# Attention with a top-32 mask and a feed-forward block: heads turned a unit sooner, lasting halves, a plain second block

## The chip, the cores and the metric

The kernel runs on one core of one Trainium2 chip. The metric is the device time of one launch, in microseconds (us); the value given for a kernel is the median of several runs. A core has five engines that each take their instructions in order: TensorE (PE in the profile, with its weight loads as PEld), VectorE (DVE), ScalarE (ACT), GpSimd (POOL) and SyncE (SP), which here issues nearly all DMAs. Waits between engines are semaphores that a framework places from what each instruction reads and writes. The program order is the one in which the Python code calls the instructions: the kernel asks for a manual schedule.

## What is computed

Everything is 32-bit floating point. The shapes are B = 8 batches, H = 8 heads, S = 576 rows, D = 64 columns a head, 512 model columns, 2048 hidden columns; the two weight matrices arrive in 64-bit floating point.

```python
scores = scale * np.matmul(q, k.transpose(0, 1, 3, 2))
kth = np.partition(scores, -top_k, axis=-1)[..., -top_k:-top_k + 1]   # top_k = 32
scores = np.where(scores >= kth, scores, -1000000000.0)
scores = scores - np.max(scores, axis=-1, keepdims=True)
attn = np.exp(scores)
attn = attn / (np.sum(attn, axis=-1, keepdims=True) + 1e-09)
x = np.matmul(attn, v)                 # then (B, H, S, D) -> (B, S, H*D)
mu, var = mean and variance of x over its last axis
xn = (x - mu) / np.sqrt(var + 1e-06) * g_ln
out = x + np.maximum(xn @ w_ch1, 0.0) @ w_ch2
```

## The kernel before

**Units and steps.** A *job* is one pair of heads of one batch with one group of query rows; a *unit* is 128 query rows of a job for both heads (two tiles of 128 x 576 scores), or the last 64 rows of both heads in one tile (a *rest* unit). There are 160 units. The main loop has one *step* for each unit and some more behind them. In step n VectorE works on unit n; the scores of unit n + 2 are made on TensorE and copied to `sc` by ScalarE; unit n - 1 is masked (`prepare`, `mask`) and exponentiated (`weigh`); unit n - 2 is turned (`turn` on TensorE, or `move` by VectorE and two DMAs); and two to four steps after a group's last unit its value product follows (`values`, `take_values`, `place`).

**Selection.** `halve` (L413 on) writes the elementwise maximum of the two halves of a score row to `hi` (L425) and the minimum to `lo` (L426). `select(u, 0..3)` takes 8 maxima at a time from `hi` (L447) and strikes them out (L433); `select(u, 1)` first puts the 8 maxima of `lo` into columns 288 to 295 of `hi` (L439). `watch` (L466, GpSimd) compares column 295 of `hi` with the threshold, so that a second pass can be run if 8 were too few. `mask` is a Relu on ScalarE (L496) and a subtraction on GpSimd (L499) for each tile; `weigh` is the exponential (L507). `hi` comes from a pool of two buffers: `halve` of unit n takes the buffer of unit n - 2 and waits until that one is given back.

**Moved units.** `move` transposes 32 x 32 squares of the exponentials on VectorE into the unit's own `sc` buffer (L538) and sends it to DRAM (`turned`, L553) some fills later (`SEND_AGE`); three steps after the unit's own, `bring` fetches it in four DMAs to `pt` (L548), which the value product reads.

**Heads.** `load` brings q and k rows in 32-column pieces; `turn_heads` transposes them on VectorE (L331) to `kT`, `qT` and `late_qT`, two buffers each; `turns` says in which step. Jobs that come back to the same heads later (`twin`) fetch them from DRAM.

**Weights.** The 64-bit weights are rebuilt in 32 pieces in steps 0 to 20: `split` (ScalarE and GpSimd, L163 to L170), `shift` (VectorE, L176), `join` (two GpSimd operations, L182 and L184). Four pieces come ahead of step 0, then one a step, later two. A join of a step's pieces stands behind the mask in GpSimd's order, and the watch stands behind the join.

**The feed-forward blocks.** Rows of x become 18 *blocks* of 256 rows, given to a list `todo` (`give`) as their attention is finished. A block has rows to turn, 64 hidden matmuls of 256 columns (L779), and a projection. `plain` projects with 32 matmuls of 512 columns (L818). `seven` does it with seven products instead of eight (56 matmuls of 256 columns, L936), with sums of the hidden rows on GpSimd (L866 to L868, L872) and four combined weight quarters: two stay in `wt`, two (*forms*) are kept in DRAM and fetched into the right half of `w2` in turn (`fetch_form`). The combined quarters are made by `form_pair` (four GpSimd subtractions of 128 x 512, L990 to L993), four times, once block 0 is through; from then on `w2` no longer holds the plain weights. Block 0 is plain, the other 17 are seven.

**The planner.** A `fill` (eight of them a step) takes matmuls from the head of `todo` as long as the head may run and the share of the step isn't used up. Up to step 21 the share is what VectorE's modelled step exceeds TensorE's by. Later `slot` spreads the listed work evenly to every later `give`:

```python
for m in sorted(gives):
    if m > n:
        even = min(even, (left - RESERVE) / (m - n))
        left += sum(b.cost() for b in gives[m])
```

Gives come in steps 9, 20, 28, 36, 43, ... 136, 148, 149, 156, 163.

Of the kernel before, what the change touches and what calls it, by code (L numbers as in the profile page):

```python
# [10 lines left out]
ALU = mybir.AluOpType  # L11
# [18 lines left out]
def compute(  # L30
# [26 lines left out]
    def pool(name, bufs, **kw):  # L57
        return ctx.enter_context(tc.tile_pool(name=name, bufs=bufs, **kw))
# [7 lines left out]
    kqpool = pool("kq", 2)  # L66
    vpool = pool("v", NV)
    scpool = pool("sc", 5)
    hipool = pool("hi", 2)
    lopool = pool("lo", 1)  # L70
    epool = pool("e", 2)
    ptpool = pool("pt", 1)
# [18 lines left out]
    def const(shape, name):  # L91
        return consts.tile(shape, FP32, tag=name, name=name)
# [14 lines left out]
    if doubt is not None:  # L107
        watched = const([P, 2, 34], "watched")
        nc.gpsimd.memset(watched[:], -1.0)
    ident = const([P, P], "ident")  # L110
    make_identity(nc, ident[:])
    half = const([P, J], "half")
# [113 lines left out]
    def join_weights(n):  # L226
        for x in batches.get(n - 1, []):
            x.join()
# [184 lines left out]
    def halve(u):  # L413

        nt = len(u.tiles)  # L420
        u.lo = lopool.tile([P, 2, HALF], FP32, tag="lo", name="lo")
        u.hi = hipool.tile([P, 2, HALF + 8 * low_rounds], FP32, tag="hi", name="hi")
        a, b = u.sc[:, 0:nt, 0:HALF], u.sc[:, 0:nt, HALF:S]
        lo, hi = u.lo[:, 0:nt], u.hi[:, 0:nt, 0:HALF]
        nc.vector.tensor_tensor(hi, a, b, ALU.max)  # L425
        nc.vector.tensor_tensor(lo, a, b, ALU.min)  # L426
# [66 lines left out]
    def mask(u, t):  # L493
        if u.e is None:
            u.e = epool.tile([P, 2, S], FP32, tag="e", name="e")
        nc.scalar.activation(  # L496
            u.e[:, t], u.sc[:, t], AF.Relu, bias=u.edge[:, t : t + 1], scale=-STEEP
        )
        nc.gpsimd.tensor_tensor(u.e[:, t], u.e[:, t], u.sc[:, t], ALU.subtract)  # L499
# [186 lines left out]
    class Block:  # L686
# [41 lines left out]
            return sum(t[1] for part in self.items() for t in part)  # L728

        def items(self):  # L730
            return self.plain() if self is blocks[0] else self.seven()

        def turn_x(self, i):
            if i == 0:
# [70 lines left out]
        def plain(self):  # L805

            hs = {}
            ps = {}
            self.o = {}

            def run(h, bank):
                hs[h] = self.relu(bank)

            def project(i, f):
                if f == 0:
                    ps[i] = product("ops")
                at = f % 2 * 2 * P + i * P
                nc.tensor.matmul(  # L818
                    ps[i][:],
                    hs[f // 2][:, at : at + P],  # L820
                    w2[:, f, :],
                    start=(f == 0),
                    stop=(f == NF - 1),
                )
                if f == NF - 1:
                    o = self.o[i] = opool.tile([P, DM], FP32, tag="o", name="o")
                    nc.scalar.copy(o[:], ps[i][:])
                    self.finish(i)
                    if i == self.n - 1:
                        plain_done[0] = now[0]  # L830

            return (
                self.rows(),
                self.hidden_items(range(NF), lambda f: (f // 2, f % 2), run),
                [
                    (
                        "project",
                        PER_ROW * DM,
                        lambda i=i, f=f: project(i, f),
                        lambda f=f: done(ready[NF + f]) and (f < NF - 1 or self.ready),  # L840
                    )
                    for f in range(NF)
                    for i in range(self.n)
                ],
            )
# [115 lines left out]
                ],  # L961
            )

    PER_ROW = 1.71e-3
    SUM_AGE, END_AGE, FETCH_AGE, STORE_AGE, LOAD_AGE = 7, 6, 10, 8, 3
    SEND_AGE, CENTRE_AGE = 2, 6
    blocks = []
    plain_done, formed, used, fetched = [None], [None], [], [0]

    def close(blk):  # L970
        while blk.ends:
            blk.ends.pop(0)()
# [3 lines left out]
    def slot_of(i):  # L976
        return w2[:, 2 * i : 2 * i + 2, 2 * P : DM]

    def form_pair(i):

        lo, hi = slice(2 * i, 2 * i + 2), slice(NF // 2 + 2 * i, NF // 2 + 2 * i + 2)
        b11, b12 = w2[:, lo, 0 : 2 * P], w2[:, lo, 2 * P : DM]
        b21, b22 = w2[:, hi, 0 : 2 * P], w2[:, hi, 2 * P : DM]
        tt = nc.gpsimd.tensor_tensor
        x = xpool.tile([P, 2, DM], FP32, tag="x", name="form")
        t1, t2 = wt[:, 0, lo], wt[:, 1, lo]
        t4, t3 = (x[:, s].rearrange("p (f n) -> p f n", f=2) for s in range(2))
        tt(t1, b12, b11, ALU.subtract)  # L990
        tt(t2, b22, t1, ALU.subtract)
        tt(t3, t2, b11, ALU.subtract)
        tt(t4, b21, t2, ALU.subtract)  # L993
        return i, x

    def keep_pair(made):
        i, x = made
        for s in range(2):
            nc.sync.dma_start(scratch[:, s, i], x[:, s])
        if i == 3:  # L1000
            formed[0] = now[0]

    def fetch_form():
        m = fetched[0]
# [6 lines left out]
    def fetch_forms(age):  # L1011
        if done(formed[0]):
            free = 4 + sum(tick[0] - x >= age for x in used)
            while fetched[0] < min(free, 8 * (len(blocks) - 1)):
                fetch_form()

    def forms(blk, k, j):
        m = 8 * (blocks.index(blk) - 1) + 4 * k + j // 2
        while fetched[0] <= m:
            fetch_form()  # L1020
        return w2[:, j, 2 * P : DM]
# [110 lines left out]
    for j in jobs[1:]:  # L1132
        before = jobs[jobs.index(j) - 1]
        made = next(n for n in range(N) if units[j.first] in due(n))
        step = max(min(before.first, made - 1), 0)
        if j.twin:
            fetches.setdefault(max(step - 1, 0), []).append(j)
        else:
            turns[step] = j
            keeps[step + 1] = j  # L1140
# [47 lines left out]
        return u.i + u.group.lag + 1 if u and u.rest and u.job.b % 2 else None  # L1188

    recips, rows_of, ends_due = {}, {}, {}  # L1190
    pairs_left, made_pair = list(range(4)), []

    def arrived(n, key, x):
        blk, i = block_of[key]
# [20 lines left out]
    for n in range(END):  # L1215
# [31 lines left out]
        if mk:  # L1247
            prepare(mk)
            for t in range(len(mk.tiles)):
                mask(mk, t)  # L1250
        if n:
            join_weights(n)
        if mk and doubt is not None:
            watch(mk)
        if plain_done[0] is not None and plain_done[0] < n - 1:
            if made_pair:
                keep_pair(made_pair.pop())
            if pairs_left:
                made_pair.append(form_pair(pairs_left.pop(0)))
        for x in ahead:  # L1260
            take_scores(x)
        if g and not quick:
# [33 lines left out]
            keep_den(ex)  # L1296
        if u:
            select(u, 1)
        if n == gives_first:
            for blk, i in rows_of.pop(n):  # L1300
                blk.stats(i)
# [126 lines left out]
```

## Time and profile before

| | us |
|---|---|
| median of 3 runs | 1618.3 (1617.16 to 1620.39) |
| the profiled execution | 1617.0 |
| its span, first to last instruction | 1615.1 |
| busy: TensorE / VectorE / ScalarE / GpSimd | 1487.4 / 1371.2 / 1057.7 / 1033.9 |

The profile is of one execution. Its page gives each engine's busy time and a row of 40 equal slices (a digit is the busy share in tenths); the waits say which instruction stood idle and what ended that; the chain of waits is followed back from the last instruction. A line such as L425 is line 425 of the kernel before. A TensorE that is shown busy can still have small stalls, since the ends of matmuls are modelled.

### The profile page before, as it was taken

The page shows a single profiled execution, that of the slowest core. Times are in us where ns is not written, and L with a number is a line of the kernel's source. Part 1 is how long each engine was busy: PE and PEld are TensorE (multiplying, and loading weights), DVE is VectorE, ACT ScalarE, POOL GpSimd, SP SyncE. Part 2 cuts the span into 40 slices and gives each one's busy share as a digit, 9 for nine tenths or more (in the row PEclk, how much of TensorE's full clock was granted, in tenths as well). Part 3 has the DMA queues.
Part 4 walks back from the last instruction along what each step waited for, and adds up shares of the span by engine and source line. Part 5 has one row for each costly group of instructions (what it writes and reads, how often), then busy time and mean ns, then how long its engine had stood idle before and what let it go on. Part 6 is the DMA issues. An engine that isn't in the chain of part 4 may idle for free.

```text
span 1615.1 us, 27577 instructions
## 1 busy us (share of the span) xinstructions
PE 1487.4 (92%) x7954; PEld 1131.2 (70%) x7954; DVE 1371.2 (85%) x3979; ACT 1057.7 (65%) x2988; POOL 1033.9 (64%) x1513
## 2 busy tenths in 40 slices
PE   3578769799999999999999999999999999999997
PEld 2346436477777677777777777777777777778886
DVE  5997998899989997999978999999999999666100
ACT  5878866667677767776767576767676676454421
POOL 6968886957566565847565756484757475647614
PEclk9879879799999999999999999999999999999999
DMA  8424763556635675565753476546666554342411
GB/s 212 115 70 138 214 154 101 159 137 189 215 103 159 181 210 153 151 185 135 204 151 112 141 200 187 157 131 178 167 176 183 170 167 142 104 120 90 138 34 48
DMA packets 387561, 241.56 MB, mean 150 GB/s; under 512 B 263492, under 2 KB 355656, under 8 KB 387400
## 3 DMA queue, kind: packets, MB, share of 16 engines
q1 hardware_dynamic: 382664, 239.11, 52.0%
q8 instruction: 66, 1.08, 0.3%
q10 hardware_dynamic: 4736, 0.59, 0.2%
q14 instruction: 95, 0.78, 0.2%
HBM read 165.15 MB, written 74.45 MB: 148 GB/s over the span
## 4 chain that ended last, share of the span: by engine, by line
PE 51%; DVE 25%; POOL 10%; DMA 5%; ACT 5%; issue 2%; SPq 1%; ACTq 0%; DVEq 0%; POOLq 0%
PE hps L779 20%; PE ops L936 15%; DVE m L447 7%; DVE hi L433 6%; PE scps L404 6%; PE av L632 5%; POOL e L499 4%; DVE sc L538 3%; DVE lo L426 2%; DVE hi L425 2%; DVE hi L439 2%; DMA pt<-turned 2%; DMA turned<-sc 2%; PE av L639 2%; PE tp L565 2%
## 5 line engine op out<-in xcount | busy, mean ns | idle before, releaser
L499 POOL TENSOR_TENSOR e<-e,sc 128x576 f32<-128x576 f32 x288 | 408.1, 1435 | 444.6 <-ACT e L496 338.9
L779 PE MATMUL hps<-xT,w 128*128 128x256 f32 x2304 | 539.0, 384 | 5.2 <-ACT xT L741 3.1
L779 PEld LDWEIGHTS hps<-xT,w 128*128 128x128 f32 x2304 | 429.9, 192 | 70.0 <-issue 7.7
L447 DVE MAX8 m<-hi 128x8 f32<-128x296 f32 (+1 forms) x1152 | 470.1, 443 | 0.5
L433 DVE MATCH_REPLACE8 hi<-m,hi 128x288 f32<-128x288 f32 (+1 forms) x864 | 377.7, 442 | 0.0
L936 PE MATMUL ops<-w,h 128*128 128x256 f32 x1360 | 321.4, 382 | 2.8 <-POOL h L872 1.4
L936 PEld LDWEIGHTS ops<-w,h 128*128 128x128 f32 x1360 | 250.8, 191 | 40.5 <-issue 3.5
L496 ACT ACTIVATE e<-sc,m 128x576 f32<-128x576 f32 x288 | 209.3, 769 | 70.4 <-PE scps L599 69.6
L507 ACT ACTIVATE e<-e,m 128x576 f32<-128x576 f32 x288 | 226.8, 790 | 43.0 <-POOL e L499 41.8
L385 ACT COPY sc<-scps 128x288 f32<-128x288 f32 x576 | 187.9, 402 | 68.6 <-POOL e L499 50.6
L425 DVE TENSOR_TENSOR hi<-sc 128x576 f32<-128x576 f32 (+1 forms) x160 | 133.9, 837 | 101.9 <-POOL watched L466 98.8
L802 ACT ACTIVATE h<-hps 128x512 f32<-128x512 f32 x144 | 87.3, 607 | 109.4 <-PE hps L779 108.8
L632 PE MATMUL av<-pt,vb 128*64 128x256 f32 (+2 forms) x1280 | 148.9, 375 | 5.5 <-DMA kept<-kT 2.4
L404 PE MATMUL scps<-kT,late_qT 64*128 64x288 f32 (+3 forms) x832 | 125.8, 414 | 9.9 <-ACT x L651 6.1
L426 DVE TENSOR_TENSOR lo<-sc 128x576 f32<-128x576 f32 (+1 forms) x160 | 134.1, 838 | 0.0
L538 DVE STREAM_TRANSPOSE sc<-e 128x512 f32<-128x512 f32 x184 | 119.2, 684 | 12.5 <-ACT e L507 7.1
L936 PE MATMUL ops<-wt,s 128*128 128x256 f32 x544 | 127.9, 380 | 1.3 <-POOL s L866 1.3
L404 PE MATMUL scps<-kT,qT 64*128 64x288 f32 x512 | 93.9, 482 | 37.3 <-DVE qT L331 34.2
L632 PEld LDWEIGHTS av<-pt,vb 128*64 128x64 f32 x1280 | 81.2, 141 | 56.0 <-issue 7.1
L439 DVE MAX8 hi<-lo 128x8 f32<-128x288 f32 x288 | 117.7, 444 | 0.0
L404 PEld LDWEIGHTS scps<-kT,late_qT 64*128 64x128 f32 (+1 forms) x832 | 72.3, 169 | 60.7 <-issue 19.2
L936 PEld LDWEIGHTS ops<-wt,s 128*128 128x128 f32 x544 | 100.5, 191 | 15.9 <-POOL s L866 2.1
(107 smaller groups left out, 1840.7 us busy)
## 6 DMA issues: line engine op xcount, KB each, us to landing
turned<-sc SPq DMA_DIRECT2D x92, 512.0 KB, 3.0
pt<-turned SPq DMA_DIRECT2D x368, 128.0 KB, 2.8
w<-forms SPq DMA_DIRECT2D x136, 256.0 KB, 4.2
vb<-in_v_dram SPq DMA_DIRECT2D x80, 288.0 KB, 4.1
raw<-in_moe_w_ch_dram SPq DMA_DIRECT2D x32, 512.0 KB, 6.1
kT<-kept SPq DMA_DIRECT2D x48, 288.0 KB, 3.5
kin<-in_k_dram SPq DMA_DIRECT2D x128, 72.0 KB, 2.7
kept<-kT SPq DMA_DIRECT2D x32, 288.0 KB, 3.1
```

The costliest lines, as they stand in the source:

```text
L385: nc.scalar.copy(u.sc[:, t, s * HALF : (s + 1) * HALF], u.made[s][t][:, 0:HALF])
L404: nc.tensor.matmul(ps[i * R : i * R + ql, o : o + width], qT[r, q0 : q0 + ql], kT[r, k0 : k0 + width], start=True, stop=True,)
L426: nc.vector.tensor_tensor(lo, a, b, ALU.min)
L433: nc.vector.match_replace(x, m[:, t, :], x, LOWEST)
L447: nc.vector.max(m[:, t, :], u.hi[:, t, 0:width])
L496: nc.scalar.activation(u.e[:, t], u.sc[:, t], AF.Relu, bias=u.edge[:, t : t + 1], scale=-STEEP)
L499: nc.gpsimd.tensor_tensor(u.e[:, t], u.e[:, t], u.sc[:, t], ALU.subtract)
L507: nc.scalar.activation(u.e[:, t], u.e[:, t], AF.Exp, bias=u.bias[:, t : t + 1], scale=-scale, accum_out=g.den[:, col : col + 1],)
L538: nc.vector.transpose(blocks.rearrange("p (j t c n) -> p j t c n", j=ni, t=2, c=J)[:, :, t], u.e[:, t, t * R : t * R + JP].rearrange("p (c ...
L632: nc.tensor.matmul(av[h * D : (h + 1) * D, 0 : g.nq], vb[:, h * (J + 1) + c, :], g.blocks[:, h, 0 : g.nq // 32, c, :], start=(c == 0), sto ...
L779: nc.tensor.matmul(ps[0][:, side * N : (side + 1) * N], w1[:, c, f * P : (f + 1) * P], self.xT[:, c, 0:N], start=(c == 0), stop=(c == NC - 1),
L936: nc.tensor.matmul(bank[name][:, 0:Q], a(j), rhs, start=first and j == 0, stop=(j == G - 1), skip_group_check=not first,)
```

## The change

- `hi` is no longer taken from a rotating pool: two lasting tiles `hi_homes` are used in turn, so that what an instruction waits for goes by the columns that it touches.
- Blocks 0 and 1 are plain (`PLAIN = 2`); the forms' indices start at block 2. `form_pair` is cut in two parts, one a step, and starts when all weights are joined, not when the plain block is done. The forms count as usable (`formed`) when all are kept and the last plain block is through.
- `move` stands behind `select(u, 1)` and no longer behind `select(u, 2)`, and `SEND_AGE` goes from 2 to 1.
- Heads that are turned from fresh loads are turned one step sooner, except for the first ones.
- `watch` stands ahead of the joins. Of the four pieces that come first, two are joined in step 0, one in step 1 and one in step 2.

```diff
-    hipool = pool("hi", 2)
...
+    hi_homes = [const([P, 2, HALF + 8 * low_rounds], f"hi{i}") for i in range(2)]
...
-        u.hi = hipool.tile([P, 2, HALF + 8 * low_rounds], FP32, tag="hi", name="hi")
+        u.hi = hi_homes[u.i % 2]
...
-            return self.plain() if self is blocks[0] else self.seven()
+            return self.plain() if blocks.index(self) < PLAIN else self.seven()
...
                 if f == NF - 1:
+                    number = blocks.index(self)
+                    if number and i == 0:
+                        close(blocks[number - 1])
                     o = self.o[i] = opool.tile([P, DM], FP32, tag="o", name="o")
                     nc.scalar.copy(o[:], ps[i][:])
                     self.finish(i)
-                    if i == self.n - 1:
+                    if i == self.n - 1 and number == PLAIN - 1:
                         plain_done[0] = now[0]
...
-    PER_ROW = 1.71e-3
+    PER_ROW, PLAIN = 1.71e-3, 2
     SUM_AGE, END_AGE, FETCH_AGE, STORE_AGE, LOAD_AGE = 7, 6, 10, 8, 3
-    SEND_AGE, CENTRE_AGE = 2, 6
+    SEND_AGE, CENTRE_AGE = 1, 6
...
-    def form_pair(i):
+    def form_pair(i, part):
...
-        x = xpool.tile([P, 2, DM], FP32, tag="x", name="form")
-        t1, t2 = wt[:, 0, lo], wt[:, 1, lo]
+        t1, t2 = wt[:, 0, lo], wt[:, 1, lo]
+        if part == 0:
+            tt(t1, b12, b11, ALU.subtract)
+            tt(t2, b22, t1, ALU.subtract)
+            return
+        x = xpool.tile([P, 2, DM], FP32, tag="x", name="form")
         t4, t3 = (x[:, s].rearrange("p (f n) -> p f n", f=2) for s in range(2))
-        tt(t1, b12, b11, ALU.subtract)
-        tt(t2, b22, t1, ALU.subtract)
         tt(t3, t2, b11, ALU.subtract)
         tt(t4, b21, t2, ALU.subtract)
...
         if i == 3:
-            formed[0] = now[0]
+            kept_forms[0] = now[0]
...
-            while fetched[0] < min(free, 8 * (len(blocks) - 1)):
+            while fetched[0] < min(free, 8 * (len(blocks) - PLAIN)):
...
-        step = max(min(before.first, made - 1), 0)
+        step = max(min(before.first, made - (1 if j.twin or made < 3 else 2)), 0)
...
-    pairs_left, made_pair = list(range(4)), []
+    pairs_left, made_pair = [(i, part) for i in range(4) for part in range(2)], []
...
+        if mk and doubt is not None:
+            watch(mk)
         if n:
             join_weights(n)
-        if mk and doubt is not None:
-            watch(mk)
-        if plain_done[0] is not None and plain_done[0] < n - 1:
+            for x in batches[-1][n + 1 : n + 2]:
+                x.join()
+        if all(map(done, ready)):
             if made_pair:
                 keep_pair(made_pair.pop())
             if pairs_left:
-                made_pair.append(form_pair(pairs_left.pop(0)))
+                made = form_pair(*pairs_left.pop(0))
+                made_pair.extend([made] if made else [])
+            if None not in (kept_forms[0], plain_done[0]) and formed[0] is None:
+                formed[0] = n
...
         if u:
             select(u, 1)
+        if moved:
+            move(ex)
...
             blk.stats(i)
-        if moved:
-            move(ex)
...
                 x.shift()
-            join_weights(0)
+            for x in batches[-1][:2]:
+                x.join()
```

More of the change, by code (lines that the diff above doesn't have):

```diff
@@ L962, in seven @@
             )
-    PER_ROW = 1.71e-3
+    PER_ROW, PLAIN = 1.71e-3, 2
     SUM_AGE, END_AGE, FETCH_AGE, STORE_AGE, LOAD_AGE = 7, 6, 10, 8, 3
-    SEND_AGE, CENTRE_AGE = 2, 6
+    SEND_AGE, CENTRE_AGE = 1, 6
     blocks = []
-    plain_done, formed, used, fetched = [None], [None], [], [0]
+    plain_done, formed, kept_forms, used, fetched = [None], [None], [None], [], [0]
     def close(blk):
@@ L1013, in fetch_forms @@
             free = 4 + sum(tick[0] - x >= age for x in used)
-            while fetched[0] < min(free, 8 * (len(blocks) - 1)):
+            while fetched[0] < min(free, 8 * (len(blocks) - PLAIN)):
                 fetch_form()
     def forms(blk, k, j):
-        m = 8 * (blocks.index(blk) - 1) + 4 * k + j // 2
+        m = 8 * (blocks.index(blk) - PLAIN) + 4 * k + j // 2
         while fetched[0] <= m:
```

## The prediction

> **What bounds the kernel now.** I read the page first (engines and slices), then the busy time by stretch, the waits, and the chain of waits inside the stretch that the change rewrites. "Step n" is one pass of the main loop; unit n is on VectorE in it. I cut the trace into steps at the starts of L425 (the max of `halve`).
>
> ```profile
> span 1615.1 us, 27577 instructions
> ...
> PE 1487.4 (92%) x7954; PEld 1131.2 (70%) x7954; DVE 1371.2 (85%) x3979; ACT 1057.7 (65%) x2988; POOL 1033.9 (64%) x1513
> ...
> PE   3578769799999999999999999999999999999997
> ...
> DVE  5997998899989997999978999999999999666100
> ```
>
> Up to slice 8 (323 us) VectorE is the full engine and TensorE has holes; from there TensorE is full to the end, and VectorE is full with it until slice 34. Two stretches, cut at steps 21, 28 and 148 (after the length: busy us of PE, PEld, DVE, ACT, POOL with counts, then the granted clock, the DMA share, GB/s):
>
> ```profile
> 244.00:318.70 74.70, 59.14 (x290) 43.02 (x289) 65.55 (x178) 47.45 (x133) 58.27 (x69) 0.84 0.42 125
> ...
> 318.70:1339.10 1020.40, 1006.91 (x5676) 775.42 (x5678) 974.83 (x2871) 716.63 (x2105) 641.71 (x1010) 1.00 0.59 166
> ```
>
> Between 318.7 and 1339.1 (steps 28 to 147) PE lacks 13.5 us and DVE 45.6 us: two engines at their limits. From 1339 to 1605 PE alone is the bound. So time is to be had before 318.7, and afterwards only as far as *both* engines are relieved. Who waits for whom, over the whole span (total, times, longest):
>
> ```profile
> DVE hi L425 <- POOL watched L466: 98.8, 42, 9.5
> ...
> PE scps L404 <- DVE qT L331: 34.2, 6, 6.9
> ```
>
> The first is `halve` waiting until the tile `hi` of two units ago is given back, whose last reader is `watch` on POOL. By stretch it is 8.4 us up to 90, some 5 us in steps 9 to 20, 8.5 us in 244 to 319, and then:
>
> ```profile
> DVE hi L425 <- POOL watched L466: 37.6, 23, 3.7
> ```
>
> in 320 to 1340; the other 39.6 us lie after 1340, where PE is the bound and the wait costs nothing. In 262 to 317 the chain of waits is POOL and nothing else:
>
> ```profile
> 284.66 0.15 POOL watched L466
> 284.81 1.25 POOL wt L990
> ...
> 286.13 1.68 POOL wt L991
> ...
> 287.88 1.68 POOL form L992
> 289.55 1.23 POOL form L993
> ...
> 293.51 2.72 POOL e L499 x2
> 296.22 0.16 POOL watched L466
> ```
>
> mask, watch, four form operations, the sums of the seven-product block, mask again: 11.6 us a step, and the DVE row starts only when watch ends. That is the one stretch where a third engine is the bound.
>
> **The change part by part.**
>
> *Second block plain, forms by halves (steps 21 to 30).* Before, block 1's projection needs the forms, made in steps 23 to 27 after block 0 is done. POOL carries there, a step, masks 2.8, watch 0.2, a pair of forms 5.9 (1.27+1.57+1.67+1.40, L990 to L993) and sums of about 1.3 x 1.5: over 10.5, against a VectorE unit of 8.8 (steps 29 to 34 are 8.8 to 9.2 us apart). After: half a pair (2.9) from step 21 on over eight steps and no sums for block 1: 6 us. POOL stops being the bound. VectorE idles 9.2 us of these 74.7; of the 3.9 before step 23, which comes from PE (24 hidden matmuls in one step), I leave 1.2. Saved: 8. The halves of steps 23 to 27 also take longer than elsewhere: L425 and L426 average 1530 and 1657 ns there, 742 ns is the median. Here stands a rule that speaks against the change: the Trainium skill, "GPSIMD Engine Reference", section 1 (Specifications), says that POOL shares its SBUF interface with VectorE instructions that have two SBUF inputs. By the rule, a halve freed from watch runs beside the mask (two inputs, 1417 ns) and eight half-forms in place of four pairs touch more units: 1.7 us (1530+1657-2x742) on each of 8 steps instead of 5, 5 us lost. By the row alone the five slow units cost 8.4 us, tied to watch ending exactly when the halve and the next form start, and would vanish: 8.4 gained. I take 0 between them, as the form work in total is the same.
>
> PE: plain costs 32 matmuls of 512 columns for 56 of 256, 2048 columns more at 216 ns a pass of 256, two passes: 3.5 us, in steps 26 to 30 where PE has holes. In exchange the work list gets ahead. The planner's rule (`slot`) spreads what is listed, plus 12 blocks of 53.4 us (2 x 0.44 + (64 + 56) x 0.438, the code's own costs), to step 148 less 4 us: (46.4 + 641 - 4)/126 = 5.42 us of matmuls a step before, (49.9 + 641 - 4)/126 = 5.45 after. Before, block 1's hidden part is used up in step 26 and steps 26 and 27 find nothing they may run, so that 24.5 us (its whole projection) are left at step 28; after, 17.6. So PE owes 6.9 us less for steps 28 to 147, 0.06 us a step. At step 148 both have 4 us left and the same four blocks to come: the end (1339 to 1605) keeps its work. This is why the large hole of PE at 282 to 318 is worth little. Eight form fetches on SP fall away; nothing waits there for one.
>
> *Joins spread, watch ahead of join (steps 0 to 2).* Before, four joins (8 x 1.27) stand ahead of the first mask and watch; step 2's halve waits 8.05 us, at 40.06. After, two joins are gone from the front, so mask and watch of unit 0 end about 32.3 and the halve doesn't ask for them. But then two joins (5.1) and the size clamp (0.6) follow on POOL, and the next instruction on VectorE, the shift L176, needs that clamp: it comes at 38.1 where it came at 41.8. Saved: 3.7, not 8. Four 0.5 us gaps at steps 12 to 19 go: 2. The 3.15 us before step 12 are kept, as the shift right behind waits for POOL until 143.0 anyway.
>
> *Heads turned one unit sooner.* 29 turns of 1.6 us (L331: 763+400+467) move one step up; nothing is added. PE's 34.2 us of waits for qT lie before 245, where PE has little to do: 0. In steps 113 to 147 they move from a full unit's step (10.7) to a rest unit's (5.6): smoother, and DVE's sum is the same. It needs a free pair of head tiles a step sooner; at the change from rest units to fresh heads (steps 72, 96) PE's scores of the same step must be first, price up to 2 us each, taken as 0.
>
> *Lasting halves.* `halve` writes columns 0 to 287, watch reads column 295: no wait. The next to wait is the low maximum of that unit (L439), one halve and one select later, 1.5+2.0 = 3.5 us more room.
>
> *Turned weights sooner.* The transpose (L538, two of 0.68) goes from behind select 2 to behind select 1, 1.9 us earlier, and its DMA leaves one fill sooner. SP then stands behind it earlier; loads, form fetches and value loads queued after it are late by what the exponent is late. For PE: its waits of over 0.3 us in 320 to 1340 sum to 17.4, of which 6.7 stand before the value matmuls (pt); these go. For DVE a new wait: I compared, for the 92 moves, the end of L507 with the end of select 1. In 44 the exponent comes later, by 45 us in total up to 1345, at most 3.0 at one. Before, DVE waited there 5 times:
>
> ```profile
>   ACT e L507: 7.1, 5
> ```
>
> So steps 28 to 147: DVE loses 37.6 us of waits at the halve and takes on between 0 and 45 at the move (a wait once paid moves the following ones, so the largest of each run counts, some 17). PE gains 6.9 + 6.7 = 13.6 at most, and loses whatever the shorter lead of VectorE starves it of. Bounds +14 and -8; I take 6, nearer to PE's row than to VectorE's, since PE is what is full in both.
>
> **Sum.** 8 + 3.7 + 2 + 6 = 19.7, and 0 in the end stretch (its PE stalls are 9.7 us; -2 to +4). The profiled execution took 1617.0 (span 1615.1), 1.3 under the median of the runs shown, 1618.3: 1597.3, **1597**.
>
> **The rivals.** (a) *Only the front gains*: steps 28 to 147 are held by two full engines, and 0 comes of them; 1617 - 13.7 = 1603. For it: DVE idles nowhere in 920 to 1050. (b) *The lead pays fully*: 13.6 from the middle, the slow halves of steps 23 to 27 shrink by 6, the end by 3: 1617 - 36 = 1581. For it: all 23 gaps of the middle are of the one kind that is removed. (c) *The move takes over, slower*: the wait for the exponent stands in front of selects 2 and 3, so it delays the next unit's threshold, mask and exponent, and repeats itself. 44 waits at their static size are 45 us; with the 37.6 saved and PE as the second bound, it decides once more than about 0.45 us a unit sticks on 44 of the 92 moves beyond what is saved: 20 us lost in the middle eat the front's 13.7. With 30 lost: 1633. Against it: ACT is 65% busy and the exponent depends on the step before, so a late DVE finds it ready. (d) The lasting tile still waits for watch (then front 8, middle 0 to 3): 1608.
>
> **Chances.** Forecast 0.55, (a) 0.18, (b) 0.10, (c) 0.11, (d) 0.06. A measurement of this kernel tells about 0.2% (3.2 us) from no change. Faster 0.85, same 0.05 (thin slices of (c) and (d)), slower 0.10. The forecast alone reaches from 1588 to 1605; with (a), and parts of (b) and (d), the range is 1583 to 1611.
>
> **What would show it.** L425 <- watched near 0 everywhere; `L538 <- ACT e` grown from 7 to 15 or 45 us; no POOL chain at 262 to 317, and step 28 reached at about 305 instead of 318.7; form operations x4 in eight steps from about 240 on, their DMAs x8, form fetches x128 instead of 136; 136 sums become 128; step 2's gap at L176 of some 4.5 us. PE 318 to 1340 again over 98% busy. Wrong if the middle changes by more than 14, or if the end stretch from step 149 on changes by more than 4.

## The result and the profile after

The median went from 1617.73 us (4 runs, 1616.88 to 1620.39) to 1594.91 us (4 runs, 1593.38 to 1599.21): ratio 0.986, 95% interval 0.9837 to 0.9884. The forecast was 1597.0 us. The profiled execution of the kernel after took 1599.21 us (span 1597.3) and is the slowest of its four; against the profiled execution of before (1617.02) that is 17.8 us less, where the medians are 22.8 apart. So the ledger below also has two later profiles of the unchanged kernel after.

The page of the kernel after, by the same rows as in the page of before (the row DVE is VectorE):

```profile
span 1597.3 us, 27330 instructions
...
PE 1489.8 (93%) x7906; PEld 1120.2 (70%) x7906; DVE 1371.9 (86%) x3979; ACT 1054.9 (66%) x2983; POOL 1023.5 (64%) x1478
...
PE   3579778999999999999999999999999999999997
...
DVE  5997999999979998999988999999999999668100
```

Total busy time is what it was (PE +2.4, VectorE +0.7). What has gone is idle time: TensorE's slices are full from slice 8 on, before from slice 9. Busy time by stretch, cut at steps 21, 28 and 148 of this kernel (length, then busy us of PE, PEld, DVE, ACT, POOL, granted clock, DMA share, GB/s):

```profile
246.70:311.50 64.80, 61.70 (x301) 44.28 (x302) 62.34 (x178) 47.13 (x129) 47.33 (x46) 0.92 0.39 124
311.50:1323.40 1011.90, 1000.13 (x5614) 761.01 (x5612) 974.79 (x2872) 713.98 (x2103) 640.90 (x999) 1.00 0.60 166
1323.40:1597.30 273.90, 259.15 (x1301) 213.80 (x1299) 121.94 (x340) 112.84 (x296) 138.74 (x230) 0.99 0.33 96
```

Steps 21 to 27 took 74.70 us and take 64.80; POOL's share of them fell from 58.27 to 47.33 us. Steps 28 to 147 took 1020.4 and take 1011.9: TensorE is 6.8 us less busy there (1006.91 to 1000.13), and its holes shrink by 1.7 (13.5 to 11.8). So the larger part of the middle's gain is work that was done earlier, not waits that went.

The chain of waits in steps 23 to 24, which was POOL and nothing else, is now a plain VectorE unit:

```profile
270.14 0.85 DVE hi L433 x2
271.00 0.73 DVE hi L439 x2
271.72 0.71 DVE m L447 x2
...
275.64 0.73 DVE hi L425
276.37 0.67 DVE lo L426
```

The waits of VectorE over the whole span (total, times, longest); L425 no longer waits for watch anywhere:

```profile
DVE st L702 <- ACT x L651: 35.7, 6, 20.2
DVE hi L439 <- POOL watched L466: 32.0, 14, 7.2
DVE sc L538 <- ACT e L507: 29.3, 15, 4.3
DVE wt L176 <- POOL wt L164: 13.7, 9, 3.4
```

and in steps 28 to 147 alone:

```profile
DVE hi L439 <- POOL watched L466: 13.3, 9, 3.5
...
DVE st L702 <- ACT x L651: 12.7, 4, 3.9
...
DVE sc L538 <- ACT e L507: 5.3, 4, 1.8
...
PE av L632 <- DMA pt<-turned: 0.9, 1, 0.9
```

The 98.8 us of waits at the halve have become 32 at the low maximum, one select later, and the wait at the move has grown from 7.1 to 29.3, but only 5.3 of it lie where VectorE matters. A third wait has grown there: L702, the statistics of a finished row of x, stands until ScalarE has placed the last value products into x (L651). In before it was, in 320 to 1340:

```profile
DVE st L702 <- ACT x L651: 3.3, 3, 1.8
```

So a VectorE that is freed from watch gets ahead and then stands four times (steps 43, 63, 75 and 87) behind what TensorE has not finished yet. All in all its idle time in steps 28 to 147 fell from 45.6 us to 37.1, which is the 8.5 us by which the stretch got shorter; its busy time stayed (974.83 and 974.79).

**The ledger.** For each kernel the starts of L425 (one a unit; it is L429 in e10 and e11) cut its profile into stretches; the table gives how many us each stretch is *shorter* than in the profile of before. Read it along columns: the same program differs by up to 2.4 us in one of them. A column shows how far VectorE has come, not the other engines (see e7).

| kernel | to step 4 | 4 to 21 | 21 to 28 | 28 to 148 | from 148 | all |
|---|---|---|---|---|---|---|
| forecast | 3.7 | 2 | 8 | 6 | 0 | 19.7 |
| after | 0.6 | -3.3 | 9.9 | 8.5 | 2.1 | 17.8 |
| after, e8 | 1.8 | -1.6 | 10.2 | 10.7 | 3.0 | 24.1 |
| after, e12 | 1.9 | -3.1 | 9.9 | 8.3 | 1.9 | 18.9 |
| e1, hi in a pool | 1.1 | -2.5 | 9.6 | 4.8 | -0.5 | 12.5 |
| e2, late move | 0.7 | -1.7 | 10.4 | 7.9 | 3.5 | 20.8 |
| e3, old turns | 0.3 | 1.6 | 10.6 | 8.1 | 2.8 | 23.4 |
| e4, one plain block | 1.4 | -2.3 | 8.5 | -1.4 | 2.6 | 8.8 |
| e5, old joins | -0.3 | -1.6 | 10.2 | 8.6 | 2.0 | 18.9 |
| e6, plain alone | 0.0 | -0.1 | 10.1 | 0.8 | 1.3 | 12.1 |
| e7, halves alone | -1.2 | 1.0 | 7.3 | -3.0 | 2.8 | 6.9 |
| e9, early turns late only | 0.2 | 1.3 | 10.4 | 10.8 | 3.1 | 25.8 |
| e10, e9 and low maxima on two sides | 0.7 | 2.0 | 10.6 | 8.3 | 2.0 | 23.6 |
| e11, low maxima on two sides | 2.3 | -1.6 | 10.2 | 10.7 | 2.1 | 23.7 |

### The profile page after: what moved, and what is told of

Same layout as the page of the kernel before. It is cut to its first block, busy times and chain, and to the rows that moved or that the text cites. A ratio compares the mean times of both kernels' runs of the same rounds, so it can differ in the third digit from the quotient of the medians.

```text
span 1597.3 us, 27330 instructions
## 1 busy us (share of the span) xinstructions
PE 1489.8 (93%) x7906; PEld 1120.2 (70%) x7906; DVE 1371.9 (86%) x3979; ACT 1054.9 (66%) x2983; POOL 1023.5 (64%) x1478
## 4 chain that ended last, share of the span: by engine, by line
PE 52%; DVE 29%; POOL 7%; ACT 6%; DMA 4%; issue 2%; SPq 1%; DVEq 0%; ACTq 0%; POOLq 0%
PE hps L779 20%; PE ops L939 16%; DVE m L447 9%; DVE hi L433 7%; PE scps L404 5%; PE av L632 4%; DVE sc L538 3%; POOL e L499 2%; DVE hi L425 2%; DVE lo L426 2%; DVE hi L439 2%; PE tp L565 2%; PE av L639 2%; ACT e L496 1%; ACT sc L385 1%
## 5 line engine op out<-in xcount | busy, mean ns | idle before, releaser
L499 POOL TENSOR_TENSOR e<-e,sc 128x576 f32<-128x576 f32 x288 | 412.9, 1452 | 436.5 <-ACT e L496 358.9
L447 DVE MAX8 m<-hi 128x8 f32<-128x296 f32 (+1 forms) x1152 | 471.0, 443 | 1.2
L939 PE MATMUL ops<-w,h 128*128 128x256 f32 x1280 | 303.5, 382 | 1.0 <-POOL h L875 1.0
L939 PEld LDWEIGHTS ops<-w,h 128*128 128x128 f32 x1280 | 236.5, 192 | 34.3 <-issue 3.5
L538 DVE STREAM_TRANSPOSE sc<-e 128x512 f32<-128x512 f32 x184 | 120.1, 684 | 35.8 <-ACT e L507 29.3
L439 DVE MAX8 hi<-lo 128x8 f32<-128x288 f32 x288 | 117.6, 443 | 32.0 <-POOL watched L466 32.0
L426 DVE TENSOR_TENSOR lo<-sc 128x576 f32<-128x576 f32 (+1 forms) x160 | 138.2, 864 | 0.0
L425 DVE TENSOR_TENSOR hi<-sc 128x576 f32<-128x576 f32 (+1 forms) x160 | 134.8, 843 | 3.0 <-ACT sc L385 3.0
L404 PE MATMUL scps<-kT,late_qT 64*128 64x288 f32 (+3 forms) x832 | 121.4, 410 | 2.1 <-ACT xT L741 1.2
L939 PE MATMUL ops<-wt,s 128*128 128x256 f32 x512 | 119.3, 380 | 1.7 <-ACT t L913 1.1
L565 PE MATMUL tp<-ident,e 128*128 128x128 f32 x416 | 70.5, 298 | 50.8 <-ACT e L507 29.8
L404 PE MATMUL scps<-kT,qT 64*128 64x288 f32 x512 | 94.3, 472 | 14.1 <-DVE qT L331 10.8
L404 PEld LDWEIGHTS scps<-kT,late_qT 64*128 64x128 f32 (+1 forms) x832 | 70.0, 168 | 53.1 <-issue 21.9
```

What stands on the lines that cost most here:

```text
L404: nc.tensor.matmul(ps[i * R : i * R + ql, o : o + width], qT[r, q0 : q0 + ql], kT[r, k0 : k0 + width], start=True, stop=True,)
L447: nc.vector.max(m[:, t, :], u.hi[:, t, 0:width])
L538: nc.vector.transpose(blocks.rearrange("p (j t c n) -> p j t c n", j=ni, t=2, c=J)[:, :, t], u.e[:, t, t * R : t * R + JP].rearrange("p (c ...
L939: nc.tensor.matmul(bank[name][:, 0:Q], a(j), rhs, start=first and j == 0, stop=(j == G - 1), skip_group_check=not first,)
```

## The experiments

The times, in three sessions, each with its own runs of before. The last column is the change against that session's before by the medians:

| kernel | median (range), us | ratio to before, 95% interval | us |
|---|---|---|---|
| session 1, before 1618.81 | | | |
| e1 | 1600.85 (1597.51 to 1604.47) | 0.9891 (0.9869 to 0.9913) | -18.0 |
| e2 | 1600.46 (1596.16 to 1601.81) | 0.9887 (0.9866 to 0.9909) | -18.4 |
| e3 | 1593.70 (1591.69 to 1594.33) | 0.9847 (0.9828 to 0.9867) | -25.1 |
| e4 | 1608.17 (1605.88 to 1610.15) | 0.9938 (0.9919 to 0.9957) | -10.6 |
| session 2, before 1617.00 | | | |
| e5 | 1596.82 (1595.49 to 1599.49) | 0.9873 (0.9855 to 0.9891) | -20.2 |
| e6 | 1604.22 (1599.51 to 1605.75) | 0.9909 (0.9892 to 0.9926) | -12.8 |
| e7 | 1611.89 (1609.99 to 1613.98) | 0.9967 (0.9956 to 0.9978) | -5.1 |
| e8, after | 1593.41 (1592.88 to 1593.87) | 0.9853 (0.9837 to 0.9869) | -23.6 |
| session 3, before 1616.15 | | | |
| e9 | 1593.04 (1591.15 to 1594.98) | 0.9861 (0.9840 to 0.9881) | -23.1 |
| e10 | 1594.22 (1592.62 to 1595.27) | 0.9865 (0.9844 to 0.9886) | -21.9 |
| e11 | 1594.82 (1593.25 to 1598.25) | 0.9875 (0.9852 to 0.9898) | -21.3 |
| e12, after | 1597.65 (1596.95 to 1598.68) | 0.9885 (0.9865 to 0.9906) | -18.5 |

The kernel after has been measured three times: 1594.91 (the result), 1593.41, 1597.65. Differences of under some 4 us between kernels of different sessions are therefore left to the ledger. Session 1 has no run of the kernel after, and a ledger row is of one execution: for e1 that is the slowest of its five (1604.47), for e2 the fastest (1596.16).

**e4: one plain block, the rest as after.**

```diff
-    PER_ROW, PLAIN = 1.71e-3, 2
+    PER_ROW, PLAIN = 1.71e-3, 1
```

> The changed kernel with only block 0 plain; forms are still made by halves from step 21 on. Theory A: forms are ready at step 29 or 30, block 1's projection waits for them longer than before, TensorE stands empty in steps 26 to 29, and the work list enters the middle with more left (24.5 or more instead of 17.6 us); POOL is still relieved in steps 21 to 28 except for block 1's sums. 1600 to 1606 us, 5 to 11 above the changed kernel. Theory B (the gain of this part is POOL's relief alone, and TensorE's hole costs nothing as the end stretch is fixed): 1594 to 1598.

Measured 1608.17, the slowest kernel with the other parts in it. The stretch of steps 21 to 27 keeps 8.5 of its 9.9 us: POOL is relieved there by the forms in halves that start at step 21. Steps 28 to 147 give 1.4 us *more* time than before, against 8.5 less. TensorE around step 28 to 30 shows why (timeline of e4, TensorE; start, length, last bracket the idle time before it and what ended it):

```profile
326.71 0.65 PE L565 MATMUL tp<-ident,e 128*128 128x128 f32 x4 [4.28 <-ACT sc L385]
...
332.33 10.86 PE L939 MATMUL ops<-w,h 128*128 128x256 f32 x48 [0.95 <-DMA w<-forms]
```

Block 1's projection may not run before the forms are usable, so TensorE stands still for 4.28 us and does the 48 matmuls at step 30. With a plain block the projection (L818) runs in steps 26 to 29, in holes. In all TensorE is idle for 8.3 us in steps 28 and 29 of e4, and for none in the kernel after. This is the forecast's work-list term and more: e4 makes its forms in eight steps and has them later than before did, where the 48 matmuls start in step 28. By the medians the second plain block is the largest single part: 23.6 or 18.5 less with it, 10.6 without.

**e6: the plain block and the forms by halves alone, all else as before.** The edit is the change's own in `items`, `form_pair`, `forms` and the main loop:

```diff
-            return self.plain() if self is blocks[0] else self.seven()
+            return self.plain() if blocks.index(self) < PLAIN else self.seven()
...
-    pairs_left, made_pair = list(range(4)), []
+    pairs_left, made_pair = [(i, part) for i in range(4) for part in range(2)], []
...
-        if plain_done[0] is not None and plain_done[0] < n - 1:
+        if all(map(done, ready)):
```

> The kernel before, with the second plain block and the forms by halves alone; everything else as before. Theory A (this part carries both the stretch of steps 21 to 27 and, through the shorter work list, about half of what steps 28 to 147 gain): 8 to 9 us by step 28, 4 to 6 more by step 148, 1603 to 1606. Theory B (it carries the stretch of steps 21 to 27 alone, the middle needs the halves freed from watch): 1608 to 1610, the ledger flat after step 28.

12.8 us, of which 10.1 lie in steps 21 to 27: theory A's time, but the middle gave 0.8 and not 4 to 6. At step 72 the kernel was still 12.1 ahead; steps 72 to 75 lost 8.6 of it. The timeline of e6, TensorE, in step 69 (667 to 675 us) and step 73 (702 to 709):

```profile
669.79 2.89 PE L632 MATMUL av<-pt,vb 128*64 128x256 f32 x16 [2.16 <-DMA pt<-turned]
...
708.60 3.41 PE L632 MATMUL av<-pt,vb 128*64 128x256 f32 x16 [3.58 <-DMA pt<-turned]
```

The value product waits for the fetch of a moved unit. The first of these cost no lead (13.0 us ahead at step 69, 13.1 at step 70); the second, 3.6 us, lies inside the loss. At VectorE the loss shows in halves that wait for watch, the longest two steps after that fetch (timeline of e6, VectorE, step 75):

```profile
720.67 1.50 DVE L425 TENSOR_TENSOR hi<-sc 128x288 f32<-128x288 f32 x1 [6.76 <-POOL watched L466]
```

The halves of steps 73 to 76 wait 12.2 us for watch in e6 and 5.1 in before. How much of this comes of the late fetch was not separated; one such wait, 2.8 us, stands ahead of it. Over 320 to 1330 this wait is 9.5 us in five places, and the halves still wait 38.8 us for watch there. So the middle is that of theory B, with a reason beside it that neither theory had named: a late transfer.

**e2: the move behind select 2, sent two fills later; the rest as after.**

```diff
-    SEND_AGE, CENTRE_AGE = 1, 6
+    SEND_AGE, CENTRE_AGE = 2, 6
...
-        if moved:
-            move(ex)
         if n == gives_first:
...
             blk.stats(i)
+        if moved:
+            move(ex)
```

> The changed kernel with the transpose of moved units behind select 2 again and its DMA two fills later. Theory A1 (the sooner transpose adds DVE waits for the exponent, 29 us in the profile of the changed kernel, that cost in the middle): faster than the changed kernel by 2 to 6 us, 1589 to 1593; the waits of the value matmuls for pt come back, some 6 us of TensorE stalls. Theory A2 (the sooner DMA is what keeps TensorE from those stalls, and the waits for the exponent only trim a lead): slower by 3 to 7 us, 1598 to 1602.

1600.46, in theory A2's range; its profile is of a run 4.3 us under that. The same place as in e6 shows the cost. Timeline of e2:

```profile
704.56 1.95 PE L632 MATMUL av<-pt,vb 128*64 128x256 f32 x16 [3.13 <-DMA pt<-turned]
```

and of the kernel after in e8:

```profile
699.99 1.95 PE L632 MATMUL av<-pt,vb 128*64 128x256 f32 x16
```

At step 74 e2 stands level with e8 (15.7 and 15.5 us ahead of before), at step 75 it is 4.1 behind it (13.4 and 17.5), and at step 148 it is 3.8 behind (17.3 and 21.1). So the early move pays at one place where a fetch was late (e12 stands there for 0.55 us, e2 for 3.13). The ledger's middle (7.9) is too near to the 8.3 of e12 to give its worth more closely than 0 to 4.

**e1: hi from the rotating pool again, the rest as after.**

```diff
-        u.hi = hi_homes[u.i % 2]
+        u.hi = hipool.tile([P, 2, HALF + 8 * low_rounds], FP32, tag="hi", name="hi")
```

> The changed kernel with hi taken again from a rotating pool of two; all else as changed. Theory A (the gain is in two stretches: about 10 us in steps 21 to 27 from the forms, about 9 us in steps 28 to 147 from halves that no longer wait for watch): the wait of the max of halve on watch comes back (some 60 to 90 us in all), the middle loses most of its gain, and the time is 1602 to 1606 us, 7 to 11 above the changed kernel's 1595. Theory B (all of the gain comes from the second block's plain projection and its work list; the halve's wait only shows the lag of TensorE): 1594 to 1597 us, no difference.

1600.85, between the ranges of the two theories. Its ratio to before (0.9891) can't be told from that of the control e12 (0.9885), so the times alone don't show what the lasting halves are worth. The ledger does: the middle gives 4.8 where the three profiles of after give 8.3 to 10.7 (8.5 in a run of after that was its slowest too), and the end nothing (-0.5 against 1.9 to 3.0). The halve's wait for watch is back at 29.0 us in 320 to 1330. Of the kernels with a second plain block, the two with a rotating pool (e1, e6) have 4.8 and 0.8 in the middle, all others 7.9 to 10.8.

**e7: the lasting halves alone, all else as before.**

```diff
-        u.hi = hipool.tile([P, 2, HALF + 8 * low_rounds], FP32, tag="hi", name="hi")
+        u.hi = hi_homes[u.i % 2]
```

> The kernel before, with the two lasting tiles for hi alone. Theory A (VectorE is freed from watch but TensorE, full in the same stretch and with the old work list, doesn't follow): the waits of L425 for watch are gone, steps 21 to 27 stay with POOL's chain, 1613 to 1617. Theory B (VectorE is the bound of the middle and the 37.6 us of waits in 320 to 1340 come back in good part): 1600 to 1608. Theory C (a halve that runs beside GpSimd's two-input operations is slower by as much as it starts sooner): 1617 to 1620.

5.1 us less, below theory A's range. The ledger has 7.3 us for steps 21 to 27, which was not foreseen, but this is a lead of VectorE alone. Freed from watch, it does select work while POOL forms and reaches step 28 7.1 us earlier; POOL's chain of masks, forms and sums ends where it did, and TensorE with it. Chain of waits of e7:

```profile
315.69 1.36 POOL e L499
...
318.40 2.29 PE scps L404 x6
```

and of before:

```profile
315.81 1.36 POOL e L499
...
318.52 2.29 PE scps L404 x6
```

Timeline of e7:

```profile
318.40 2.29 PE L404 MATMUL scps<-kT,late_qT 64*128 64x288 f32 x6 [4.43 <-ACT x L651]
320.62 12.80 PE L936 MATMUL ops<-w,h 128*128 128x256 f32 x48
```

and of before:

```profile
318.52 2.29 PE L404 MATMUL scps<-kT,late_qT 64*128 64x288 f32 x6 [4.30 <-ACT x L651]
320.74 11.49 PE L936 MATMUL ops<-w,h 128*128 128x256 f32 x48
```

The 48 matmuls of block 1's projection start 0.1 us from where they did, and by step 32 VectorE's lead is down to 0.3 us. So POOL is the bound of steps 21 to 27, halves freed or not. From step 32 to step 148 the halves alone then win 3.8 us for the 37.6 us of waits that they remove, the plain block alone (e6) 0.1, and the whole change 8.5 to 10.9: together they give more than the sum of the two. The early transfer is no condition for that (e2: 7.9 in the middle).

**e5: the joins and the watch as before, the rest as after.**

```diff
-        if mk and doubt is not None:
-            watch(mk)
         if n:
             join_weights(n)
-            for x in batches[-1][n + 1 : n + 2]:
-                x.join()
+        if mk and doubt is not None:
+            watch(mk)
...
-            for x in batches[-1][:2]:
-                x.join()
+            join_weights(0)
```

> The kernel after, with the joins as before: all four first pieces joined in step 0, the watch behind the join. Theory A (the joins' new place gives nothing, since the shift L176 waits for the POOL size clamp L164 that stands behind the same GpSimd work): 1594 to 1597, start of step 3 within 1 us of the kernel after; the 7.4 us that the halve of step 2 gains in the kernel after are gone, and the wait at L176 in step 2 with them. Theory B (spread joins are worth the 3.7 us of the forecast): 1598 to 1600.

Theory A fell, though the time lies in its range: 1596.82 against 1593.41 of the control in the same session, with ranges that do not overlap (1595.49 to 1599.49, 1592.88 to 1593.87), and the halve of step 3 stands 2.5 us later than in before where the control has it 1.0 earlier. The spread joins, with the watch ahead of them, are worth about 3.4 us by the medians; the edit takes both back, so it can't tell one from the other. And the 7.4 us at the halve of step 2, which the expectation gave to the joins, are there in e5 too (7.6): either the lasting halves (e7: 7.2) or the spread joins (e1, without lasting halves: 6.7) give them, and it is the next wait, at the shift, that tells the kernels apart.

**e3: the old turns, the rest as after.**

```diff
-        step = max(min(before.first, made - (1 if j.twin or made < 3 else 2)), 0)
+        step = max(min(before.first, made - 1), 0)
```

> The changed kernel with heads turned in the step of before. Theory A: the turn moved in steps 12 to 18 onto the steps that already carry a transpose of a moved unit (15.1 us beside 8.2, before 12.8 beside 10.1), which cost some 3 us by step 21; in the middle it changes little. So 1590 to 1594, 1 to 5 us faster than the changed kernel. Theory B (turning sooner is what smooths steps 113 to 147, where a turn now stands in a rest unit's step): slower by 3 to 6 us, 1598 to 1601.

1593.70, as fast as the change by the time, and unlike it in one column: steps 4 to 21 gain 1.6 us instead of losing 1.6 to 3.3. The three kernels with old turns in these steps and all other new parts (e3, e9, e10: 1.3 to 2.0) stand apart from all with early turns (after three times, e1, e2, e4, e5, e11: -1.6 to -3.3).

**e9: early turns only where they fall into a rest unit's step.**

```diff
-        step = max(min(before.first, made - (1 if j.twin or made < 3 else 2)), 0)
+        step = max(min(before.first, made - (1 if j.twin or made < 110 else 2)), 0)
```

> The kernel after, with the heads turned one unit sooner only for jobs whose first scores are made from step 110 on (where the turn falls into a rest unit's step); all earlier turns at the old place. Theory A (the early turn costs 1 to 2 us in steps 2 to 21, since it falls into steps that also carry a move, and gains 2 to 3 in steps 113 to 125): step 28 at -12 and step 125 at -22 or more against the kernel before, time 1590 to 1592. Theory B (TensorE is full there, and what VectorE gains in 113 to 125 is lost again by step 148; the early turn is worth nothing anywhere): 1592 to 1594, as the kernel with the old turns.

The fastest kernel of its session: 4.6 us (0.29%) under the control, whose range lies wholly above it, and with e3 the best that was found. Its step 125 is 23.1 us ahead of before, as theory A says. But of the 2.7 us that the late turns gain over e3 between steps 113 and 125 (3.0 against 0.3), 1.9 are gone by step 148, where TensorE is the bound (e3 gains another 1.5, e9 loses 0.4): there theory B holds. What carries the difference to the control lies in steps 4 to 20. The waits at the shift, which is used only up to step 20, in e9:

```profile
DVE wt L176 <- POOL wt L164: 9.4, 6, 3.4
```

and e12, the control:

```profile
DVE wt L176 <- POOL wt L164: 13.6, 9, 3.4
```

**e11 and e10: low maxima on alternating sides.** Columns 8 to 295 hold the halves; the eight low maxima go to the right for two units and to the left for the next two, so L439 does not meet the watch of two units ago. The maxima of the first and last select also come from a pool of three buffers of their own, before from one of four. e11 has this beside the change, e10 beside e9.

```diff
-                o = HALF + 8 * r
+                o = (0 if u.left else LEFT + HALF) + 8 * r
...
+        u.left = LEFT > 0 and u.i // 2 % 2 == 1
```

> The kernel after, with the low maxima on alternating sides alone, early turns kept. Its difference to the control is what the wait L439 for watch costs, 32 us of it in all: theory A 0 to 2 us, theory B 3 to 5 us, theory C 0 with the waits found again at the move (L538) or at the shift (L176).

> As the kernel before it in this list, and the eight low maxima lie to the right of the halves for two units and to the left for the next two, so that L439 writes columns that watch read four units ago and doesn't wait for it. Theory A (the waits of L439 for watch, 12 to 13 us in 320 to 1340, stand where TensorE is the bound, and cost 0 to 2): 1589 to 1592. Theory B (they are paid as the waits at the halve were, about 5 us of time for 24 of waits): 2 to 4 less, 1587 to 1589. Theory C (the freed low maximum only moves the wait to the next instruction that needs ScalarE or GpSimd): no difference.

The wait at L439 is gone in both. Of e11 (its L544 is L538 of the others):

```profile
DVE sc L544 <- ACT e L513: 27.7, 12, 5.9
DVE sc L544 <- issue: 16.2, 3, 9.5
```

and of the control e12:

```profile
DVE hi L439 <- POOL watched L466: 31.6, 15, 7.2
DVE sc L538 <- ACT e L507: 29.3, 15, 4.3
...
DVE sc L538 <- issue: 6.5, 1, 6.5
```

31.6 us of waits removed bring a ledger equal to e8's (23.7 and 24.1 in all). The median is 2.8 under its control, but e10 is 1.2 *above* e9, where theory B asked for 2 to 4 less; neither is more than the kernel after differs from itself. Some 10 us of the wait are found again at the move (16.2 against 6.5). In 320 to 1330 alone, e11 (its L708 is L702 of the others) has

```profile
DVE st L708 <- ACT x L657: 17.8, 4, 5.4
```

and e12

```profile
DVE st L702 <- ACT x L651: 13.3, 4, 3.9
DVE hi L439 <- POOL watched L466: 13.0, 10, 2.6
```

The move waits there for 12.3 us in e11 and 5.3 in e12. So of the 13.0 us at L439, 4.5 are found again at the statistics and 7.0 at the move: VectorE waits 30.1 us in e11 and 31.6 in e12. That is theory C, with one place more than it named. Whether these waits cost nothing because TensorE is the bound there (theory A), the runs don't decide.

**e8 and e12: the kernel after again.**

> The kernel after without an edit, as control beside the others on this chip: 1593 to 1597 by its first runs. The profile taken of it first was of its slowest run (1599.2); a second profile is to say whether the middle (steps 28 to 147) gives back 8.5 us against the kernel before, or some 12.

> The kernel after without an edit, as control for the three others: 1593 to 1596.

The second and third profile give 10.7 and 8.3 us for the middle. e12 came out above its expected 1596; what makes sessions of one program differ by 4 us was not found.

## Why the prediction was right, step by step

*Second block plain: 8, measured 9.9 to 10.2.* The mechanism was right. VectorE's idle time in these steps fell from 9.2 us to 2.5, by 6.7 where 8 was taken; the rest is shorter halves. The zero that was put between +8.4 (slow halves vanish) and -5 (more units touched) was the small miss: L425 and L426 in steps 23 to 27 average 1311 and 1205 ns, against 1531 and 1657, so 5 x 0.67 = 3.4 us came back. So the runs stand between the figure from the rule of the Trainium skill, "GPSIMD Engine Reference", section 1 (Specifications), and that from the row, nearer to the row. Both effects are there: with half-forms and halves still tied to watch (e6, and e1) the averages are 967 and 1178 ns, 5.2 us less than before, and freeing the halves gives 1.9 of it back, as the rule has it. "A third engine is the bound" stood: in e7, with POOL's load unchanged, its chain ends within 0.1 us of where it did.

*Joins spread: 3.7, measured 0.6 to 1.9 by step 4.* The joins and the watch are worth up to what was forecast: e5 stands 2.3 to 3.6 us behind the three profiles of after at step 3, 0.9 to 2.2 at step 4. The failed step is "the size clamp comes at 38.1". Timeline of the kernel after:

```profile
32.64 1.52 DVE L425 TENSOR_TENSOR hi<-sc 128x576 f32<-128x576 f32 x1
33.52 0.70 POOL L466 TENSOR_TENSOR watched<-hi,m 128x2 f32<-128x2 f32 x1
34.18 1.78 POOL L182 TENSOR_TENSOR size<-size,wt 128x512 uint32<-128x512 uint32 x1
...
39.96 0.61 POOL L164 TENSOR_SCALAR size<-size 128x512 f32<-128x512 f32 x1
...
40.61 0.43 DVE L176 TENSOR_SCALAR size<-size 128x512 uint32<-128x512 uint32 x1 [5.77 <-POOL size L164]
```

The clamp is at 39.96. Watch and join beside the freed halve take 0.70 and 1.78 where they take 0.20 and 1.26 alone: 1.0 us. The mask in front starts at 30.79, and at 29.80 in e3, where the turn stands elsewhere: 1.0 more. The forecast had put both other parts, halves and turns, at nothing in this stretch; e7 shows 1.2 us lost by step 4 with the halves alone. The gap at L176 (forecast 4.5) is 5.77.

*Gaps of steps 12 to 19: 2; measured -1.6 to -3.3.* This is the part of the sum that had the wrong sign. The term itself held (1.3 to 2.0 in e3, e9 and e10). The failed step is "Heads turned one unit sooner: 0": only the changeovers at steps 72 and 96 were priced, not the steps that a turn is moved *into*. In steps 4 to 20 the early turn makes the shift reach POOL's clamp too soon (4.2 us more waits at L176, e12 against e9) and moves the halves beside POOL's joins: L425 and L426 sum to 34.4 us in e8 and 29.9 in e3, of which the shifts, 18.5 against 23.4, give 4.9 back. Net 3 to 5 us lost.

*Steps 28 to 147: 6; measured 8.3 to 10.7.* The work-list term was right: 6.9 us less TensorE work forecast, 6.8 in the profile of after and 8.3 in that of e8 (998.59 busy). The term of 6.7 for the value product was not: those stalls went (av waits 0.9 us), but my count of all TensorE stalls over 0.3 us in 320 to 1330, taken as start to start less the matmul's own passes, falls only from 17.4 to 14.4, 14.3 (e8) and 15.8 (e12), as the transposes L565 behind ScalarE's copies grow from 3.2 to 8.1 (e8). The wait for the exponent at the move, expected at 15 to 45 us, is 5.3 there, so rival (c) never began. "The largest of each run counts, some 17" was too much. What had no term at all is VectorE's longer wait at the statistics: of the 39.4 us that the halve no longer waits in steps 28 to 147, 13.3 stand at L439, 9.4 more than before at L702 and 5.3 at the move.

*End: 0 (-2 to +4); measured 1.9 to 3.0.* Kernels with lasting halves have 1.9 to 3.5 there, the two without -0.5 and 1.3. So the 39.6 us of waits said to cost nothing cost about 2.

*Rivals.* (a), 1603, is what one gets with only one of the two middle parts (e6 1604.22, e4 1608.17), not with both. (b) asked for 13.6 in the middle and 6 more from the slow halves: half of the latter came. (d) is refuted by the missing L425 wait. The three profiles of the kernel after sum to 17.8, 24.1 and 18.9; the forecast's 19.7 lies among them, made up of three terms too small and two too large. That the sum came so near is in part luck: in the profile of after, 8.4 us too much in the two and 6.5 too little in the three cancel.

## What to carry to other kernels

With two engines full side by side, removing the waits of one buys little until the other has less to do in that stretch: move its work earlier, into holes, first, and then check that the transfers keep up with the new lead. When an instruction is moved to another step, price the steps that it is moved into, one by one. A wait that goes on a slack engine or stands in front of another wait is worth little: e11 removed 31.6 us of waits for at most 2.8 us, and most of them stood at the next two places. A lead of one engine is not yet a gain: e7 had 7.1 us at step 28 and 0.3 at step 32, as the engine that was the bound had not moved.

## What the runs showed of the hardware

Two-input element-wise operations of VectorE and GpSimd stretch each other, and the profile shows this as longer instructions, not as idle time. A step with a join behind the watch in the kernel after:

```profile
162.26 1.09 DVE L425 TENSOR_TENSOR hi<-sc 128x576 f32<-128x576 f32 x1
162.81 1.67 POOL L184 TENSOR_TENSOR w<-wt,sign 128x512 f32<-128x512 f32 x1
163.28 1.82 DVE L426 TENSOR_TENSOR lo<-sc 128x576 f32<-128x576 f32 x1
```

Alone the halves take 0.74 us each and this join 1.26.

In e8 a 128x576 halve takes 741 ns with no GpSimd instruction beside it (98 times, 726 to 757), and 1435 ns where a mask L499 ran beside it for more than half of its length (28 times, 747 to 1965). The worst is 741 + 1224, no more than one mask of about 1400. That agrees with the Trainium skill, "SBUF — State Buffer", section "Who interferes with whom": the port pair is locked for a whole instruction, and whoever comes second stands until the first is done. By that rule an instruction with one SBUF input outside the two-port modes isn't touched, and the maxima (L447 over 288 columns, 442 ns alone, 440 beside the mask, 207 times) and the transposes (L538, 690 and 684) are not. The shift L176, one input, is: 427 ns alone (twice), 876 beside the mask (13 times, up to 1621); by the rule it would have to run in a two-port mode, which no run here shows.

The granted TensorE clock in steps 21 to 27 is 0.92 where it was 0.84, with TensorE busy for 61.70 of 64.80 us instead of 59.14 of 74.70; which of the two follows from the other was not tried.
